# Linear attention and a gated FFN in one Trainium2 kernel: Q's weights loaded as two halves of the rows instead of four quarters, and the first passes of Q0 and Q1 each cut in two

## The chip, the cores and the metric

The kernel runs on one core of a Trainium2 chip. The core has five engines with queues of their own: TensorE (PE in the profile; PEld are its weight loads), VectorE (DVE), ScalarE (ACT), GpSimd (POOL) and SyncE (SP), which here only issues transfers. Each engine works off its own instructions in order; they wait for each other, and for transfers (DMA), by semaphores. The metric is the device time of one execution in microseconds (us), lower is better.

## The reference

One sequence of 2048 tokens with 576 features goes through a layer norm, and the sum of three parts is the output: the input itself, linear attention, and an FFN with a gelu gate. Both inner parts take the same normalised tokens.

```
xn = layernorm(x)                                  # 2048 x 576
q, k, v = split(xn @ wqkv)                         # 32 heads of 18
pq, pk = phi(q), phi(k)                            # phi(t) = t + 1 for t > 0, else exp(t); + 1e-6
num = pq @ (pk^T v);  den = pq . sum(pk) + 1e-6    # per head
out = x + (num / den) @ wo + (gelu(xn @ w_gate) * (xn @ w_up)) @ w_down   # FFN width 4608
```

## The kernel before

The 2048 tokens are 16 tiles of 128. A tile n of x is loaded (`load_x`, L163), its statistics are taken (VectorE's `bn_stats`, L310, and `bn_aggr`, L330; rstd on ScalarE, L334 and L335), it is normalised into `xn` (`ln_norm`, L342 to L351), and brought with features on the partitions into `xnT`, for tiles 0 to 3 by TensorE transposes (L363) and two copies (`tp_copy`, L368: half by ScalarE, half by VectorE), for the others by transposing transfers (`dma_transposes`, L371). Tiles 0 and 1 are transposed first with the mean alone removed, into `xcT`; rstd is multiplied in behind the product (`raw`, L456 and L458). For these two, the normalised tile follows by a transposing transfer as well.

K and Q of a tile (`_Token`, L437) are products of that tile with 576 columns of `wqkv`. The 576 rows of the contraction are four blocks of 128 (index `kt`, 0 to 3) and an end of 64. TensorE runs as two halves of 64 rows, called LO (rows 0 to 63) and HI (64 to 127); each output of 576 columns is two banks of 288 (index `i` below), and each bank gets both halves. `_Unit` (L248) does that in two passes. In the first pass (`rows`, L264) LO works for bank 0 and HI for bank 1, kt 0 to 3: 4 pairs of matmuls. Then the halves swap the banks, which needs a "turn": an empty instruction on GpSimd (`swap`, L270) that waits for the first pass, and for which the second pass (`p2`, L277) waits. The second pass has kt 0 to 3 and the end (kt 4, tile `w_ends`): 5 pairs. All matmuls of these units and of the FFN's units are recorded under L259. The FFN's gate and up products for the first 512 tokens (units g0 to g13, class `_Raw`) are woven into the same stretch, and K4 to K15 follow among them.

Order of the work. The engines' queues are filled by a planner: every piece of work is a `step` (L302) with an engine, an assumed time, a rank, what it comes after, and an earliest time (`ready`); `in_order` (L69) plays them through and emits them in the order in which they begin. TensorE's order is written out by hand in `line` (L493), where `t2` is tile 2's transposes, `K0` and `Q0` are first passes, and a point is the second pass of the oldest unit that has had its first:

```
line = "t0 t1 K0 K1 . . Q0 Q1 . t2 . K2 Q2 . t3 . K3 Q3 .".split()
```

The transfers of SyncE's queue are written out too (the calls at L209 to L223, then `loads`, L597). The planner's assumed landings stand in `X_AT`, `W_AT` and `DMA_FREE` (L373 to L375). `LATER` (L47) is the earliest time at which it plans the exp of the K tiles that were put aside raw (K0, K1, K3), and 16 us after it that of the Q tiles (Q0, Q1, Q3).

Loads at the start. SyncE issues x tile 0, K's weights (`load_w_main(1)`, one load of 128 partitions by 4 blocks by 576 columns), and then Q's weights in four quarters (`load_w_quarter`, L170), each 64 partitions by 4 blocks by 288 columns, x tile 2 between the first and the second. The first two quarters (LO with columns 0 to 287, HI with 288 to 575) are just what a first pass reads, the last two the rest of what a second pass reads. ScalarE issues x tile 1. GpSimd issues the ends of K's weights at once, and the two ends of Q's (`load_w_ends`, L175) as steps behind two small pieces of its own work. x tile 3 follows on SyncE. GpSimd's queue also holds `x_twin` (L354), a copy of a tile's last 64 features that the transposes need, and the two first loads of the FFN's ends (`load_ends`, L191).

After this stretch (to about 57 us) come the Gram product of K (`gram`, L628), the attention matrix, and then four rounds of FFN units, down projection and output.

Of the kernel before, what the change touches and what calls it, by code (L numbers as in the profile page):

```python
# [14 lines left out]
P = 128  # L15
HP = 64
S = 2048
D = 576
# [25 lines left out]
LAG = 0.08  # L44
RAW_T = ("K0", "Q0", "K1", "Q1", "K3", "Q3")
HEAD_T = RAW_T + ("K2", "Q2")
LATER = 40.0  # L47
CENTRED = (0, 1)
LEAD = 5


# [37 lines left out]
def kernel(  # L89
# [73 lines left out]
    def load_x(n0, cnt, on=nc.sync):  # L163
        on.dma_start(x_sb[:, n0:n0 + cnt, 0:D], x_view[:, n0:n0 + cnt, :])  # L164

    def load_w_main(which):
        c = slice(which * D, (which + 1) * D)
        nc.sync.dma_start(wqkv_sb[:, 0:4, c], A_wqkv[0:4 * P, c].rearrange("(kt p) c -> p kt c", p=P))  # L168

    def load_w_quarter(which, rows, half):  # L170
        c = which * D + half * HALF
        view = A_wqkv[0:4 * P, c:c + HALF].rearrange("(kt p) c -> p kt c", p=P)
        nc.sync.dma_start(wqkv_sb[rows, 0:4, c:c + HALF], view[rows])  # L173

    def load_w_ends(which, halves):  # L175
        for i in halves:
            c = which * D + i * HALF
            nc.gpsimd.dma_start(w_ends[(HI, LO)[i], which, :], A_wqkv[512:576, c:c + HALF])

    def load_w_last(which, rows):  # L180
        c = slice(which * D, (which + 1) * D)
# [31 lines left out]
    nc.vector.memset(warm[:], 0.0)  # L213
    nc.vector.memset(x_sb[:, 1, 0:1], 0.0)
    load_x(1, 1, nc.scalar)
    load_w_ends(1, (0, 1))
    load_w_main(1)
    load_w_quarter(0, LO, 0)
    load_x(2, 1)
    load_w_quarter(0, HI, 1)  # L220
    load_w_quarter(0, LO, 1)
    load_w_quarter(0, HI, 0)
    load_x(3, 1)  # L223

    act_acc = const.tile([P, 1], F32, name="act_acc")
# [22 lines left out]
    class _Unit:  # L248
# [12 lines left out]
                start=start, stop=stop, skip_group_check=True,  # L261
            )

        def rows(self):  # L264
            for kt in self.first:
                self.mm(0, LO, kt, kt == self.first[0], False)
                self.last = self.mm(1, HI, kt, kt == self.first[0], False)

# [101 lines left out]
    def dma_transposes(n):  # L370
        nc.sync.dma_start_transpose(xnT[:, :, n * P:(n + 1) * P], xn[:, n, :])  # L371

    X_AT = [3.40, 3.80, 7.30, 9.70]  # L373
    W_AT = {"K": 6.00, "Q": 7.90}
    DMA_FREE = 9.8  # L375

    places = {}

# [4 lines left out]

    for n in range(4, NS, 2):
        load(("x", n), 0.58, 295, 9.0, [], lambda n=n: load_x(n, 2), ready=6.0)
    for half, behind in enumerate((("twin", 1), ("mean", 1))):
        step(("w_ends", half), "POOL", 0.6, -9.0, [behind], lambda half=half: load_w_ends(0, (half,)))
    for part, turn in enumerate(("K1", "Q0")):
        step(("ends", part), "POOL", 0.7, 3.0, [("turn", turn)], lambda part=part: load_ends(0, nc.gpsimd, (part,)))

    for n in range(NS):
        first = 1.5 * n if n < 4 else 9.0 + 3.0 * (n - 4)
        both = n // 2 * 2
        after_x = [("x", both)] if n >= 4 else []
        x_at = X_AT[n] if n < 4 else 12.6 if n < 8 else 2.1 * both + 3.0
        if n < 4:
            step(("twin", n), "POOL", 0.2, first, [], lambda n=n: x_twin(n, 1), ready=10.1 if n == 3 else x_at)
        elif n == both:
            step(("twin", n), "POOL", 0.25, first, after_x, lambda n=n: x_twin(n, 2), ready=max(2.6 * n + 3.0, 14.6))
        twin = ("twin", n if n < 4 else both)  # L400
        if n != 1:
            for h in range(2):
                step(("stats", n, h), "DVE", 0.42, first, after_x + [("xnT", 2, 1)] * (n == 3 and h) + [("phi", "Q2")] * (n in (4, 5)) + [("phi", "K5")] * (n in (12, 13)), lambda n=n, h=h: ln_half(n, h), ready=x_at)
            step(("aggr", n), "DVE", 0.2, first, [("stats", n, 0), ("stats", n, 1)], lambda n=n: ln_aggr(n), tail=0.05)
        if n in CENTRED:
            if n:
                step(("sum", n), "ACT", 0.78, first - 3.0, [], lambda n=n: act_sum(n), ready=x_at)
                step(("mean", n), "POOL", 0.54, first - 3.0, [("sum", n)], lambda n=n: act_mean(n), tail=-0.27)
                step(("aggr", n), "ACT", 0.95, first + 2.0, [("mean", n), ("xnT", 1, 0)], lambda n=n: act_square(n))
            mean = ("mean", n) if n else ("aggr", n)  # L410
            step(("centre", n), "DVE", 0.45, first - 0.5, [mean, twin], lambda n=n: centre(n), tail=0.05)
        if n not in (1, 2) and n < 6:
            step(("rstd", n), "ACT", 0.5, first - 2.0 * (n == 3), [("aggr", n)], lambda n=n: ln_rstd(n, 1))
        elif n == both:
            m = min(n, 1) if n < 6 else n
            step(("rstd", n), "ACT", 0.46, first, [("aggr", m), ("aggr", m + 1)], lambda m=m: ln_rstd(m, 2))
            if n == 2:
                steps[("rstd", 1)] = _Step("none", 0.0, first, [("rstd", 2)], lambda: None, 0.0, 0.0)
        ready = [("rstd", n if n < 6 else both), twin]
        if NORM[n] == "A":  # L420
            step(("bias", n), "POOL", 0.27, first, ready[:1], lambda n=n: ln_bias(n))
            ready.append(("bias", n))
        on, took = ("ACT", 0.92) if NORM[n] == "A" else ("DVE", 0.45)
        if n < HEAD:
            late = n in CENTRED
            step(("norm", n), on, took, 2.5 if late else first, ready + [("tp", n)] * late, lambda n=n: ln_norm(n), tail=0.05)
            step(("tp", n), "PE", 0.2, 0, [("centre" if late else "norm", n)], lambda n=n: transposes(n), tail=0.15)
            for i, copied in enumerate((0.44, 0.30)):
                step(("xnT", n, i), "DVE" if i else "ACT", copied, first - 1.0, [("tp", n)], lambda n=n, i=i: tp_copy(n, i), tail=0.02)
            steps[("xnT", n)] = _Step("none", 0.0, first, [("xnT", n, 0), ("xnT", n, 1)], lambda: None, 0.0, 0.0)  # L430
            if late:
                load(("xnU", n), 1.25, 80, first + 2, [("norm", n)], lambda n=n: dma_transposes(n))
        else:
            step(("norm", n), on, took, first, ready, lambda n=n: ln_norm(n), tail=0.05)
            load(("xnT", n), 1.25, 80, first + 2, [("norm", n)], lambda n=n: dma_transposes(n))
# [54 lines left out]
                out=hT[:, self.f:self.f + NF + 1:NF, :], in_=ps_all[:, self.two[0]:self.two[0] + 2, :],  # L490
            )

    line = "t0 t1 K0 K1 . . Q0 Q1 . t2 . K2 Q2 . t3 . K3 Q3 .".split()  # L493
    follow = [f"g{i}" for i in range(LEAD)]
    for i in range(12):
        follow += [f"K{i + 4}"] + ([f"g{i + LEAD}"] if i + LEAD < RAW else [])
# [27 lines left out]

    def p2_step(u):
        n = int(u.name[1:])
        pe(("p2", u.name), u.t2, [("turn", u.name)], u.unit_p2, ready=9.4 if u.name == "Q0" else 0.0)
        if u.name[0] in "KQ":
            later = u.name in RAW_T
            if later:  # L530
                step(("raw", u.name), *(("DVE", 0.82) if u.name == "Q1" else ("ACT", 0.75 if n < 2 else 0.66)), u.at, [("p2", u.name), ("rstd", n or 2)] + [("norm", 3)] * (u.name == "Q1") + [("xnT", 2, 0)] * (u.name == "Q0"), u.body.raw)
            ready, rank = ((LATER, 60.0) if u.name[0] == "K" else (LATER + 16.0, 70.0)) if later else (0.0, u.at - 3.0 * (u.name == "K4"))
            held = [("xnT", 3, 0)] if u.name == "K2" else []
            step(("exp", u.name), "ACT", 0.70, rank, [("raw" if later else "p2", u.name)] + held, u.body.exp, ready=ready)
            step(("clamp", u.name), "DVE", 0.25, rank + 1, [("exp", u.name)], u.body.clamp)
            step(("phi", u.name), "DVE", 0.76, rank + 1, [("clamp", u.name)], u.body.phi, tail=0.05)
            owner[tuple(u.body.banks)] = [("raw" if later else "phi", u.name)]
        else:
            step(("out", u.name), "ACT", 1.05, u.at, [("p2", u.name)], u.body.out)
            owner[tuple(u.body.two)] = [("out", u.name)]  # L540

    clock = 5.5
    for name in line:
        if name == ".":
            p2_step(pending.pop(0))
            continue
        kind, n = name[0], int(name[1:])
        if kind == "t":
            two = (tp_banks[n], tp_banks[n] + 1)
            steps[("tp", n)].after = steps[("tp", n)].after + owner.get(two, [])  # L550
            pe(("tp", n), 0, [], None)
            owner[two] = [("xnT", n, 0), ("xnT", n, 1)]
            if name == "t0":
                pe("spin", 0.27, [], lambda: row_spin(5))
            continue
        u = _Chain()
        u.name, u.at = name, clock
        if kind in "KQ":
            u.body = _Token(kind, n, head_banks if name in HEAD_T else banks)
            b = u.body.banks  # L560
            after = [("xnT", n)]
            t1, u.t2 = 0.49, 0.615
            u.p1 = u.body.unit.rows
            u.swap = u.body.unit.swap
            u.unit_p2 = u.body.unit.p2
            at = W_AT[kind]
        else:
            u.body = _Raw(n)
            b = u.body.two
# [5 lines left out]
            u.unit_p2 = lambda body=u.body: body.unit.p2()  # L575
            at = 0.0
        after += owner.get(tuple(b), [])
        pe(("p1", name), t1, after, u.p1, ready=at)
        step(("turn", name), "POOL", 0.06, clock, [("p1", name)], u.swap, tail=0.05)
        clock += t1 + u.t2  # L580
        pending.append(u)
    while pending:
        p2_step(pending.pop(0))
# [428 lines left out]
```

## Time and profile before

| | us |
|---|---|
| median of 3 runs (508.46, 509.66, 509.67) | 509.66 |
| the profiled execution, whole | 508.54 |
| its span in the profile | 506.8 |
| TensorE busy in the span | 502.5 |

The profile is one further execution. All times in it count from the start of the span. A row of the timeline gives start and length in us, engine, source line, operation, what it writes from what, shapes and count; in brackets stands how long the engine had been idle before it, and what ended that. "SPq" is the issue of a transfer on SyncE. A row of the windows gives the length of a stretch, each engine's busy time in it, the granted clock of TensorE (1.00 throughout), the share of the transfer engines and GB/s.

### The profile page before, as it was taken

How to read it: one execution, taken by the hardware profiler on the slowest of the kernel's cores; microseconds unless marked ns; L12 is line 12 of the kernel's file. 1: busy time of each engine (PE TensorE's matmuls, PEld its weight loads, DVE VectorE, ACT ScalarE, POOL GpSimd, SP SyncE). 2: the span in 40 equal slices, each digit the busy share in tenths (PEclk: the TensorE clock that was granted, in tenths of full speed). 3: DMA queues.
4: the chain of work that ended last, by engine and by line, in shares of the span. 5: the costliest groups of instructions: out<-in, count | busy, mean ns of one | idle time of the engine just before them, and what ended most of it. 6: DMA issues, size and time to landing. Idle time of an engine off the chain costs nothing.

```text
span 506.8 us, 11207 instructions
## 1 busy us (share of the span) xinstructions
PE 502.5 (99%) x4765; PEld 304.8 (60%) x4765; DVE 230.8 (46%) x481; ACT 150.4 (30%) x263; POOL 11.2 (2%) x36
## 2 busy tenths in 40 slices
PE   9999999999999999999999999999999999999997
PEld 7666784446777444445777444445777444445774
DVE  4779896773002665553002665553102665553100
ACT  5678734325001522332001432333001432232000
POOL 4100100000000000000000000000000000000000
PEclk9999999999999999999999999999999999999999
DMA  9998916993201455653000455653000455640000
GB/s 218 236 240 188 313 51 196 269 258 96 71 13 35 136 152 170 170 153 107 12 13 31 140 151 166 173 155 108 13 12 29 143 149 162 175 107 14 13 12 25
DMA packets 115227, 61.76 MB, mean 122 GB/s; under 512 B 24642, under 2 KB 115082, under 8 KB 115178
## 3 DMA queue, kind: packets, MB, share of 16 engines
q1 hardware_dynamic: 114842, 60.63, 45.6%
q8 instruction: 37, 0.61, 0.5%
q0 software_dynamic: 192, 0.28, 0.2%
q10 hardware_dynamic: 144, 0.15, 0.1%
q14 instruction: 12, 0.10, 0.1%
HBM read 53.60 MB, written 2.36 MB: 110 GB/s over the span
## 4 chain that ended last, share of the span: by engine, by line
PE 97%; DMA 1%; SPq 1%; issue 0%; DVE 0%
PE ps_all L259 62%; PE ps_all L927 28%; PE ps_all L628 3%; PE ps_all L932 3%; DMA wqkv_sb<-in_A_wqkv_dram 1%; PE ps_all L915 0%; PE ps_all L636 0%; SPq L173 0%; PE ps_all L655 0%; SPq L164 0%; PE ps_all L867 0%; SPq L168 0%; PE ps_all L363 0%; DVE res L941 0%; PE ps_all L674 0%
## 5 line engine op out<-in xcount | busy, mean ns | idle before, releaser
L259 PE MATMUL ps_all<-xnT,wg 64*128 64x512 bf16 x1152 | 273.7, 376 | 0.0
L259 PE MATMUL ps_all<-xnT,wu 64*128 64x512 bf16 x1152 | 273.1, 376 | 0.0
L259 PEld LDWEIGHTS <-wg 64*128 64x128 bf16 x1152 | 108.3, 94 | 66.5
L259 PEld LDWEIGHTS <-wu 64*128 64x128 bf16 x1152 | 108.2, 94 | 65.5
L820 DVE TENSOR_TENSOR hT<-ps_all,gl 128x512 bf16<-128x512 f32 x130 | 89.8, 691 | 104.2 <-ACT gl L819 104.1
L927 PEld LDWEIGHTS <-hT 128*128 128x128 bf16 x1152 | 110.8, 98 | 30.9 <-issue 1.3
L819 ACT ACTIVATE gl<-ps_all 128x512 f32<-128x512 f32 x130 | 77.6, 597 | 164.1 <-PE ps_all L259 163.7
L941 DVE TENSOR_TENSOR res<-ps_all,x_sb 128x288 bf16<-128x288 f32 (+2 forms) x32 | 13.8, 455 | 146.3 <-PE ps_all L932 88.1
L927 PE MATMUL ps_all<-wd_a,hT 128*128 128x288 bf16 (+2 forms) x512 | 68.3, 286 | 0.0
L259 PE MATMUL ps_all<-xnT,wr 64*128 64x512 bf16 x288 | 54.9, 376 | 0.0
L927 PE MATMUL ps_all<-hT 128*128 128x288 bf16 (+2 forms) x384 | 52.4, 286 | 0.0
L841 ACT ACTIVATE gl<-ps_all 128x288 f32<-128x288 f32 x24 | 9.2, 410 | 121.4 <-PE ps_all L259 118.9
L927 PE MATMUL ps_all<-wd_m,hT 128*128 128x288 bf16 (+2 forms) x256 | 36.8, 286 | 0.0
L259 PEld LDWEIGHTS <-xnT 64*128 64x128 bf16 x504 | 26.6, 94 | 6.9 <-ACT xnT L368 0.6
L259 PEld LDWEIGHTS <-wr 64*128 64x128 bf16 x288 | 14.2, 94 | 16.3
L932 PE MATMUL ps_all<-m_sb,pqT 128*128 128x288 bf16 (+2 forms) x128 | 20.9, 286 | 0.0
L259 PE MATMUL ps_all<-wqkv_sb,xnT 64*128 64x288 bf16 x256 | 19.7, 283 | 0.1
L628 PE MATMUL ps_all<-hT,xn 128*128 128x288 bf16 x128 | 16.2, 286 | 0.0
L489 ACT CAST hT<-ps_all 128x1024 bf16<-128x1024 f32 x14 | 14.1, 1010 | 4.9 <-PE ps_all L259 4.8
L628 PEld LDWEIGHTS <-xn 128*128 128x128 bf16 x128 | 12.4, 98 | 3.7 <-issue 0.7
L310 DVE BATCH_NORM_STATS2 stats<-x_sb 128x6 f32<-128x288 bf16 x30 | 12.2, 440 | 5.2 <-DMA x_sb<-in_A_x_dram 5.2
L932 PEld LDWEIGHTS <-pqT 128*128 128x128 bf16 x128 | 12.4, 98 | 3.3
(98 smaller groups left out, 246.8 us busy)
## 6 DMA issues: line engine op xcount, KB each, us to landing
wg<-in_B_w_gate_dram SPq DMA_DIRECT2D x72, 256.0 KB, 3.0
wu<-in_B_w_up_dram SPq DMA_DIRECT2D x72, 256.0 KB, 3.6
wd_a<-in_B_w_down_dram SPq DMA_DIRECT2D x4, 576.0 KB, 8.6
wr<-in_B_w_gate_dram SPq DMA_DIRECT2D x35, 64.0 KB, 3.3
wr<-in_B_w_up_dram SPq DMA_DIRECT2D x35, 64.0 KB, 2.9
out_dram<-res SPq DMA_DIRECT2D x15, 144.0 KB, 1.8
x_sb<-in_A_x_dram SPq DMA_DIRECT2D x6, 288.0 KB, 4.9
hT<-in_B_w_down_dram SPq DMA_DIRECT2D x4, 432.0 KB, 5.4
```

Of the source, the lines that this page charges most:

```text
L259: return nc.tensor.matmul(self.outs[i], lhsT=self.lhs(i, rows, kt), rhs=self.rhs(i, rows, kt), start=start, stop=stop, skip_group_check=True,)
L310: nc.vector.bn_stats(out=ln_raw[n][:, h, :], in_=x_sb[:, n, h * HALF:(h + 1) * HALF])
L489: nc.scalar.copy(out=hT[:, self.f:self.f + NF + 1:NF, :], in_=ps_all[:, self.two[0]:self.two[0] + 2, :],)
L628: nc.tensor.matmul(ps_all[:, two[hf], :HALF], lhsT=xn[:, n, kt * P:(kt + 1) * P], rhs=pk[:, n, hf * HALF:(hf + 1) * HALF], start=(n == gra ...
L819: nc.scalar.activation(out=gl[:], in_=ps_all[:, b[0], :], func=ACT.Gelu_apprx_tanh)
L820: nc.vector.tensor_tensor(out=hT[:, GUB * k + i, :], in0=ps_all[:, b[1], :], in1=gl[:], op=ALU.mult)
L841: nc.scalar.activation(out=e[:, :HALF], in_=acc, func=ACT.Exp)
L927: nc.tensor.matmul(self.acc(hf), lhsT=hT[:, f, j * P:(j + 1) * P], rhs=wd(f)[:, self.parts[hf]], start=(f == 0 and not paired), stop=False ...
L932: nc.tensor.matmul(self.acc(hf), lhsT=pqT[:, c, self.ts], rhs=m_sb[:, c, self.parts[hf]], start=False, stop=(paired and c == 3), skip_grou ...
L941: nc.vector.tensor_tensor(out=self.res[:, hs], in0=self.acc(hf), in1=x_sb[:, self.n, hs], op=ALU.add)
```

## The change

Q's weights come as two loads of 128 partitions and 576 columns, kt 0 and 1 in one, kt 2 and 3 in the other. x tile 2 is issued before both, and the two ends of Q's weights after them, on SyncE's queue. As each half holds both banks' columns but only half of the contraction, the first passes of Q0 and Q1 are cut: `Q0a`, `Q1a` take kt 0 and 1, `Q0b`, `Q1b` kt 2 and 3, and tile 2's transposes stand ahead of Q0's second pass instead of behind it. The turns of Q0 and Q1 follow the second halves. GpSimd issues both first loads of the FFN's ends behind K1's turn; the plan's assumed landings and `LATER` have other values, so the planner puts some of VectorE's and ScalarE's work in another order.

```diff
-LATER = 40.0
+LATER = 38.0
+WQ_PARTS = ((0, 1), (2, 3))
...
-    def load_w_main(which):
+    def load_w_main(which, kts=slice(0, 4)):
         c = slice(which * D, (which + 1) * D)
-        nc.sync.dma_start(wqkv_sb[:, 0:4, c], A_wqkv[0:4 * P, c].rearrange("(kt p) c -> p kt c", p=P))
...
+        view = A_wqkv[0:4 * P, c].rearrange("(kt p) c -> p kt c", p=P)
+        nc.sync.dma_start(wqkv_sb[:, kts, c], view[:, kts, :])
+
+    def load_w_ends(which, on):
+        for i, rows in enumerate((HI, LO)):
             c = which * D + i * HALF
-            nc.gpsimd.dma_start(w_ends[(HI, LO)[i], which, :], A_wqkv[512:576, c:c + HALF])
+            on.dma_start(w_ends[rows, which, :], A_wqkv[512:576, c:c + HALF])
...
-    load_w_ends(1, (0, 1))
+    load_w_ends(1, nc.gpsimd)
     load_w_main(1)
-    load_w_quarter(0, LO, 0)
     load_x(2, 1)
-    load_w_quarter(0, HI, 1)
-    load_w_quarter(0, LO, 1)
-    load_w_quarter(0, HI, 0)
+    for kts in WQ_PARTS:
+        load_w_main(0, slice(kts[0], kts[-1] + 1))
+    load_w_ends(0, nc.sync)
     load_x(3, 1)
...
-        def rows(self):
-            for kt in self.first:
+        def rows(self, kts=None):
+            for kt in self.first if kts is None else kts:
...
-    X_AT = [3.40, 3.80, 7.30, 9.70]
-    W_AT = {"K": 6.00, "Q": 7.90}
-    DMA_FREE = 9.8
+    X_AT = [3.40, 3.80, 6.90, 9.60]
+    W_AT = {"K": (6.00,), "Q": (7.90, 8.90)}
+    DMA_FREE = 9.6
...
-    for half, behind in enumerate((("twin", 1), ("mean", 1))):
-        step(("w_ends", half), "POOL", 0.6, -9.0, [behind], lambda half=half: load_w_ends(0, (half,)))
-    for part, turn in enumerate(("K1", "Q0")):
-        step(("ends", part), "POOL", 0.7, 3.0, [("turn", turn)], lambda part=part: load_ends(0, nc.gpsimd, (part,)))
+    for part in range(2):
+        step(("ends", part), "POOL", 0.6, 3.0, [("turn", "K1")], lambda part=part: load_ends(0, nc.gpsimd, (part,)))
...
-    line = "t0 t1 K0 K1 . . Q0 Q1 . t2 . K2 Q2 . t3 . K3 Q3 .".split()
+    line = "t0 t1 K0 K1 . . Q0a Q1a Q0b Q1b t2 . . K2 Q2 . t3 . K3 Q3 .".split()
...
+        if name[-1] == "b":
+            u = pending[-1 if name[:2] == pending[-1].name else -2]
+            pe(("p1", u.name), 0.245, [], lambda u=u: u.p1(WQ_PARTS[1]), ready=W_AT["Q"][1])
+            step(("turn", u.name), "POOL", 0.06, clock, [("p1", u.name)], u.swap, tail=0.05)
+            continue
...
+        if name[-1] == "a":
+            pe(("p1a", u.name), 0.245, after, lambda u=u: u.p1(WQ_PARTS[0]), ready=at)
```

More of the change, by code (lines that the diff above doesn't have):

```diff
@@ L164, in load_x @@
         on.dma_start(x_sb[:, n0:n0 + cnt, 0:D], x_view[:, n0:n0 + cnt, :])
-    def load_w_main(which):
+    def load_w_main(which, kts=slice(0, 4)):
         c = slice(which * D, (which + 1) * D)
-        nc.sync.dma_start(wqkv_sb[:, 0:4, c], A_wqkv[0:4 * P, c].rearrange("(kt p) c -> p kt c", p=P))
[L170 to L176, printed above, removed]
+        view = A_wqkv[0:4 * P, c].rearrange("(kt p) c -> p kt c", p=P)
+        nc.sync.dma_start(wqkv_sb[:, kts, c], view[:, kts, :])
+    def load_w_ends(which, on):
+        for i, rows in enumerate((HI, LO)):
             c = which * D + i * HALF
-            nc.gpsimd.dma_start(w_ends[(HI, LO)[i], which, :], A_wqkv[512:576, c:c + HALF])
+            on.dma_start(w_ends[rows, which, :], A_wqkv[512:576, c:c + HALF])
     def load_w_last(which, rows):
@@ L396 @@
         if n < 4:
-            step(("twin", n), "POOL", 0.2, first, [], lambda n=n: x_twin(n, 1), ready=10.1 if n == 3 else x_at)
+            step(("twin", n), "POOL", 0.2, first, [("turn", "Q1")] * (n == 3), lambda n=n: x_twin(n, 1), ready=10.1 if n == 3 else x_at)
         elif n == both:
@@ L526, in p2_step @@
         n = int(u.name[1:])
-        pe(("p2", u.name), u.t2, [("turn", u.name)], u.unit_p2, ready=9.4 if u.name == "Q0" else 0.0)
+        pe(("p2", u.name), u.t2, [("turn", u.name)], u.unit_p2)
         if u.name[0] in "KQ":
@@ L546 @@
             continue
-        kind, n = name[0], int(name[1:])
+        kind, n = name[0], int(name[1:].rstrip("ab"))
         if kind == "t":
@@ L555 @@
             continue
+        if name[-1] == "b":
[3 more added lines that the diff above has]
+            continue
         u = _Chain()
-        u.name, u.at = name, clock
+        u.name, u.at = name[:2] if name[-1] == "a" else name, clock
         if kind in "KQ":
-            u.body = _Token(kind, n, head_banks if name in HEAD_T else banks)
+            u.body = _Token(kind, n, head_banks if u.name in HEAD_T else banks)
             b = u.body.banks
@@ L565 @@
             u.unit_p2 = u.body.unit.p2
-            at = W_AT[kind]
+            at = W_AT[kind][0]
         else:
@@ L577 @@
         after += owner.get(tuple(b), [])
-        pe(("p1", name), t1, after, u.p1, ready=at)
-        step(("turn", name), "POOL", 0.06, clock, [("p1", name)], u.swap, tail=0.05)
         clock += t1 + u.t2
+        if name[-1] == "a":
+            pe(("p1a", u.name), 0.245, after, lambda u=u: u.p1(WQ_PARTS[0]), ready=at)
+        else:
+            pe(("p1", name), t1, after, u.p1, ready=at)
+            step(("turn", name), "POOL", 0.06, u.at, [("p1", name)], u.swap, tail=0.05)
         pending.append(u)
```

## The prediction

> **What bounds the kernel now.** I read the page's first part, the chain of waits in order of time, the waits of the first 18 us, and the timeline of the first 16 us.
>
> ```profile
> span 506.8 us, 11207 instructions
> PE 502.5 (99%) x4765; PEld 304.8 (60%) x4765; DVE 230.8 (46%) x481; ACT 150.4 (30%) x263; POOL 11.2 (2%) x36
> ```
>
> TensorE (PE) is busy for 99% of the span. The change leaves its instructions in number and shape as they are, so it can only win or lose idle time. The chain (start, length, what) shows where that time is:
>
> ```profile
> 4.46 5.56 DMA wqkv_sb<-in_A_wqkv_dram
> 10.06 0.83 PE ps_all L259 x9
> ...
> 14.30 42.81 PE ps_all L259 x504
> 57.11 3.78 PE ps_all L628 x30
> 60.90 8.25 PE ps_all L628 x66
> ```
>
> Until 10.02 the end hangs on a transfer, the last quarter of Q's weights. From 14.30 PE is one piece but for a hole at 60.7. The weight loads (PEld) say who ended each hole of the head; the columns are total us, times, longest:
>
> ```profile
> PEld L259 <- ACT xnT L368: 0.6, 2, 0.4
> PEld L259 <- issue: 0.6, 2, 0.4
> PEld L259 <- POOLq L270: 0.3, 1, 0.3
> PEld L363 <- DVE xn L348: 0.2, 1, 0.2
> ```
>
> These are weight-load gaps; the matmuls run on through part of each, so they add up to more than PE loses. The pace of undisturbed work comes from the timeline (start, length):
>
> ```profile
> 11.63 1.65 PE L259 MATMUL ps_all<-wqkv_sb,xnT 64*128 64x288 bf16 x24
> ...
> 13.10 0.30 PE L259 MATMUL ps_all<-w_ends,xnT 64*128 64x288 bf16 x2
> ```
>
> Twelve pairs start between 11.63 and 13.10: 0.1225 us a pair. A first pass (4 pairs) is 0.49, a half 0.245, a second pass (5 pairs) 0.61.
>
> **The change, part by part.** *The loads.* Four quarters become two halves; x tile 2 moves ahead of all of them; the ends of Q's weights move from GpSimd to SyncE, behind them.
>
> ```profile
> 1.73 0.74 SPq L173 DMA_DIRECT2D wqkv_sb<-in_A_wqkv_dram  x1
> 2.51 0.59 SPq L164 DMA_DIRECT2D x_sb<-in_A_x_dram  x1
> ...
> 3.15 1.93 SPq L173 DMA_DIRECT2D wqkv_sb<-in_A_wqkv_dram  x3
> ...
> 5.13 0.60 SPq L164 DMA_DIRECT2D x_sb<-in_A_x_dram  x1
> ```
>
> SyncE issues as many as before: four quarters of 0.64 to 0.74 go, two halves and two ends come, near 0.6 each, so x tile 3 still goes out near 5.1. What changes is the rate, in GB/s at the row's end:
>
> ```profile
> 4.00:5.00 1.00, 1.00 (x11) 0.81 (x8) 0.84 (x3) 0.97 (x4) 0.86 (x3) 1.00 1.08 384
> 6.00:9.50 3.50, 3.50 (x62) 2.51 (x58) 1.62 (x5) 1.49 (x4) 0.81 (x3) 1.00 1.16 207
> ```
>
> Between 4 and 5 us K's weights come in, 128 partitions of 1152-byte rows: 384. Between 6 and 9.5 it is the quarters, 64 partitions of 576-byte rows: 207. A half has the shape of K's load. K's issue at 1.27 takes 4.5 us to land:
>
> ```profile
> wqkv_sb<-in_A_wqkv_dram SPq DMA_DIRECT2D x1, 576.0 KB, 4.5
> ```
>
> So K lands at 5.8. Behind it come x2 (147 kB), two halves of 295, the ends (74), x3 (147). At 384 they land at 6.2, 7.0, 7.7, 8.1 (the ends at 207), 8.5; at 207, the other bound, at 6.5, 7.9, 9.4, 9.7, 10.4. A bound below is not reasonable: fewer, longer rows have no row here that runs under 207. I take 384, the row of the same shape.
>
> [...]
>
> *The wait of x2.*
>
> ```profile
> 8.03 0.82 DVE L310 BATCH_NORM_STATS2 stats<-x_sb 128x6 f32<-128x288 bf16 x2 [1.31 <-DMA x_sb<-in_A_x_dram]
> 8.06 0.23 POOL L354 COPY x_sb<-x_sb 128x64 bf16<-128x64 bf16 x1 [2.00 <-PE ps_all L259]
> 8.10 1.58 PEld L259 LDWEIGHTS <-xcT 64*128 64x128 bf16 x28 [0.27 <-POOLq L270]
> ...
> 9.81 0.81 DVE L348 TENSOR_SCALAR xn<-x_sb,mv,rstd 128x640 bf16<-128x640 bf16 x2 [0.72 <-ACT rstd L335]
> ```
>
> VectorE waits for x2 until 8.03. GpSimd's queue has x2's copy in front of K1's turn, so PE waits too: K1's second pass could follow K0's at 7.96 and starts at 8.10. With x2 at 6.2 to 6.5 the statistics start when VectorE is free, at 6.72 (its copy at 6.39 takes 0.32), 1.3 earlier, and norm 2 (the first at 9.81, 0.45 long) ends near 8.95 instead of 10.25.
>
> *PE.* K1's second pass 7.96, Q0a 8.57, Q1a 8.82, Q0b 9.07, Q1b 9.31. The halves are there (7.0 and 7.7; the slow bound, 7.9 and 9.4, is priced below). Tile 2's transposes, 0.15 long, at 9.56 find norm 2 done. Q0's and Q1's second passes take 1.22, to 10.93; the ends, landed at 8.1 to 9.7, are needed at 10.2. K2 and Q2's first passes 0.98, K2's second 0.61, tile 3's transposes 0.15, Q2's second 0.61: K3 at 13.28, against 14.30. That is 4.21 behind the start of Q0b.
>
> *What is late next.* K3 also needs VectorE's copy of tile 3:
>
> ```profile
> 10.54 0.44 DVE L310 BATCH_NORM_STATS2 stats<-x_sb 128x6 f32<-128x288 bf16 x1
> ...
> 11.38 0.75 ACT L456 ACTIVATE pq<-ps_all,rstd 128x576 bf16<-128x576 f32 x1
> ...
> 12.13 0.30 ACT L334 ACTIVATE rstd<-mv,eps_ln 128x1 f32<-128x1 f32 x1
> ...
> 12.75 0.45 DVE L348 TENSOR_SCALAR xn<-x_sb,mv,rstd 128x640 bf16<-128x640 bf16 x1 [0.66 <-ACT rstd L335]
> ...
> 13.11 0.81 DVE L458 TENSOR_SCALAR pq<-ps_all,rstd 128x576 bf16<-128x576 f32 x1
> ...
> 13.84 0.32 DVE L368 COPY xnT<-ps_all 128x320 bf16<-128x320 bf16 x1
> ```
>
> On ScalarE Q0's copy (11.38), then tile 3's rstd, then norm 3, Q1's copy and xnT's on VectorE, then K3: 14.30 − 11.38 = 2.92. The changed order keeps this sequence, and Q0's copy now starts when Q0's second pass has drained, its last pair starts 0.49 behind 9.71 and takes 0.30: 10.5. K3 then starts near 13.45: 0.8 gained, 0.2 of PE's possible 1.0 stays a wait. With the halves at 207 GB/s Q0b waits until 9.44, and K3 is at 9.44 + 4.21 = 13.65: 0.65.
>
> *New waits.* Q0b and Q1b wait for the second half; behind them on PE stands everything. GpSimd issues both first FFN ends between K1's turn (7.56) and Q0's (needed 9.5), two at 0.52 and gaps of 0.3, done by 9.2. K2's turn stands behind x3's copy; x3 has until 11.4. If that cover were gone, each would cost PE one for one.
>
> *LATER 38.* Q0's exp goes ahead of K13's, and its two VectorE steps into a hole:
>
> ```profile
> 56.16 0.62 DVE L468 TENSOR_SCALAR phi_e<-phi_e 128x576 bf16<-128x576 bf16 x1 [1.28 <-ACT phi_e L465]
> ...
> 57.56 0.33 DVE L468 TENSOR_SCALAR phi_e<-phi_e 128x576 bf16<-128x576 bf16 x1
> 57.93 0.76 DVE L474 SCALAR_TENSOR_TENSOR pq<-pq,phi_e 128x576 bf16<-128x576 bf16 x1
> ...
> 60.09 0.76 DVE L474 SCALAR_TENSOR_TENSOR hT<-ps_all,phi_e 128x576 bf16<-128x576 f32 x1
> ```
>
> K15's phi ended at 60.85, and the Gram product waited until 60.90. Its 30 matmuls before that, at 0.1225, could go on at 60.73: 0.17 lost. 0.33 + 0.76 = 1.1 leave the queue ahead of K15's phi, which comes near 59.75, and PE, 0.8 earlier, asks at 59.9. Without this edit the 0.8 would be lost here. I count 0.15 gained; from both sides 0 and 0.17.
>
> **The sum**: 0.8 + 0.15 = 0.95 us. The profiled execution took 508.54 us (span 506.8 and 1.7 around it): 507.6. The executions shown stand in two pairs, 508.46 and 508.54, 509.66 and 509.67; the profiled one is of the lower, the median of the upper, and nothing in this trace shows the 1.15 between. I take the middle of the pairs, 509.1, less 0.95: 508.1.
>
> **Rivals.**
> *The halves land no sooner.* For: the load is shared with whatever else is queued. Against: 384 in the same shape, and fewer bytes ahead. K3 starts 4.21 behind the landing's release; from 10.05 on nothing is left. Before, the last quarter landed at 10.02: gain 0, with the Gram hole 0.15: 509.0.
> *The gain is taken back by weights of the FFN units.* For: PE comes 0.8 sooner to loads at near 290 GB/s:
>
> ```profile
> 10.50:12.50 2.00, 2.00 (x40) 1.55 (x38) 1.38 (x5) 1.89 (x5) 0.23 (x1) 1.00 1.12 290
> ```
>
> Against: these start behind x1's transposing transfer, which waits for norm 1, itself about 1.3 earlier. What is left then is 0 to 0.4: 508.9.
> *Slower: norm 6 behind x8.* In the changed order VectorE's norm 6 stands behind all of x8's first statistics, not behind one half:
>
> ```profile
> 22.76 0.46 DVE L310 BATCH_NORM_STATS2 stats<-x_sb 128x6 f32<-128x288 bf16 x1 [1.45 <-DMA x_sb<-in_A_x_dram]
> 23.14 0.43 DVE L348 TENSOR_SCALAR xn<-x_sb,mv,rstd 128x640 bf16<-128x640 bf16 x1
> ...
> 24.79 2.53 SPq L371 DMA_TRANSPOSE xnT<-xn  x2
> 31.44 0.67 PE L259 MATMUL ps_all<-wqkv_sb,xnT 64*128 64x288 bf16 x8
> ```
>
> Three more steps of 0.45, 0.21 and 0.41 put its end near 24.6 for the same landing, just in time for its transpose at 24.79. It decides from x8 landing about 23: each us beyond holds SyncE's queue, the transposes of 6 and 7 and the weights behind, and K6 at 31.44. Two us cost 509.1 − 0.95 + 2 = 510.2. Against: x8 is issued about a us sooner.
>
> **How the numbers follow.** Forecast 0.71 (own range 507.3 to 509.0: the pair that the median falls in, and 0.65 to 1.0); no sooner 0.10; taken back 0.08; slower 0.11. 0.3% of 509.66 is 1.53, about what a measurement of this kernel can tell from no change: faster means below 508.13. The forecast lies at that edge: a median of the lower pair (507.6) is over it, one of the upper (508.7) is not: 0.36 and 0.35. The two cases of a lost gain are within. Of the slower case 0.03 stays within and 0.08 goes over 511.2, with more than one late landing. Faster 0.36, same 0.56, slower 0.08. The range leaves out the slower case and the ends: 507.3 to 509.7.
>
> **What would show it.** Right: the chain leaves the DMA before 8.6 us; x2's statistics start near 6.7; no wait on GpSimd's turn before K1's second pass; K3 near 13.5, ended by xnT's copy; PE unbroken at the Gram product. Wrong: a matmul of Q0b waiting for a DMA after 9.1 us; PE holes between 15 and 57 us; K3 at 14.3.

## The result and the profile after

The changed kernel takes 507.31 us (median of 10 executions, 507.05 to 507.74), the kernel before, run beside it, 508.44 (10 executions, 507.94 to 509.83). The ratio of the means is 0.9972, 95% interval 0.9962 to 0.9982: a gain of 0.9 to 1.9 us. The executions of before form two groups, seven at 507.94 to 508.88 (median 508.31) and three at 509.66 to 509.83; the changed kernel has one group. So the gain has two parts: 1.0 from the lower group (508.31 to 507.31), and the upper group, which is gone (3 of 10 executions, 1.4 each, 0.4 in the mean).

The page of the changed kernel, first two lines; its profiled execution took 507.23 us.

```profile
span 505.5 us, 11200 instructions
PE 500.9 (99%) x4765; PEld 304.7 (60%) x4765; DVE 230.8 (46%) x481; ACT 150.4 (30%) x263; POOL 10.4 (2%) x34
```

The span is 1.3 shorter. The chain of the changed kernel (start, length, what):

```profile
0.81 2.65 DMA x_sb<-in_A_x_dram
...
5.99 3.45 PE ps_all L255 x52
9.59 2.82 PE ps_all L255 x46
12.55 43.40 PE ps_all L255 x514
55.95 11.87 PE ps_all L630 x96
```

It leaves the DMA with x tile 0, at 3.46, and no longer with Q's weights at 10.02. From 5.99 it stays on TensorE, the Gram product is one piece, and the hole at 60.7 is gone. Who ended TensorE's holes before 18 us in the changed kernel (weight loads; total us, times, longest):

```profile
PEld L359 <- DVE xn L321: 0.6, 1, 0.6
PEld L255 <- ACT xcT L364: 0.2, 1, 0.2
PEld L255 <- ACT xnT L364: 0.2, 1, 0.2
```

No GpSimd turn is left, and no "issue": in the kernel before, those were two waits that ended 0.04 behind the landings of the last quarter (10.02) and of the second end (10.55). The stages of the head, timeline of the changed kernel:

```profile
5.26 0.44 PE L239 MATMUL ps_all<-warm 64*128 64x128 bf16 x10
...
6.35 0.80 DVE L306 BATCH_NORM_STATS2 stats<-x_sb 128x6 f32<-128x288 bf16 x2
6.54 2.59 PEld L255 LDWEIGHTS <-xcT 64*128 64x128 bf16 x44 [0.20 <-ACT xcT L364]
...
7.67 0.67 PE L255 MATMUL ps_all<-wqkv_sb,xcT 64*128 64x288 bf16 x8
...
8.12 0.80 DVE L344 TENSOR_SCALAR xn<-x_sb,mv,rstd 128x640 bf16<-128x640 bf16 x2 [0.72 <-ACT rstd L331]
...
8.28 1.16 PE L255 MATMUL ps_all<-wqkv_sb,xcT 64*128 64x288 bf16 x16
...
10.25 0.74 ACT L450 ACTIVATE pq<-ps_all,rstd 128x576 bf16<-128x576 f32 x1 [0.22 <-PE ps_all L255]
...
13.05 1.49 PEld L255 LDWEIGHTS <-xnT 64*128 64x128 bf16 x26 [0.19 <-ACT xnT L364]
```

These are the ten fillers between the transposes of tiles 0 and 1, x2's statistics, K1's first pass (6.54), K1's second (7.67), norm 1 and 2, the cut first passes of Q0 and Q1 as one run of 16 matmuls from 8.28, Q0's copy, and K3 (13.05). The same three points in the kernel before:

```profile
5.33 0.72 PE L243 MATMUL ps_all<-warm 64*128 64x128 bf16 x10
...
6.83 1.00 PEld L259 LDWEIGHTS <-xcT 64*128 64x128 bf16 x18 [0.26 <-ACT xcT L368]
...
14.27 1.49 PEld L259 LDWEIGHTS <-xnT 64*128 64x128 bf16 x26 [0.39 <-ACT xnT L368]
```

From K1's first pass to K3 it was 7.44 and is 6.51: the head gains 0.93. The other 0.29 of K3's 1.22 was there before any changed transfer mattered: the same ten fillers take 0.72 in one execution and 0.44 in the other (last section).

The rate of the loads in the changed kernel (windows; GB/s at the end):

```profile
4.00:5.00 1.00, 0.63 (x11) 0.46 (x8) 0.85 (x3) 0.97 (x4) 0.39 (x2) 1.00 1.09 389
...
6.00:8.70 2.70, 2.70 (x44) 2.33 (x46) 1.94 (x7) 2.36 (x7) 1.08 (x3) 1.00 1.13 296
```

The halves come at 296, between the quarters' 207 and the 384 of K's load; why not at 384, no run shows.

### The profile page after: what moved, and what is told of

Its sections match the earlier page's. It is cut to its first block, busy times and chain, and to the rows that moved or that the text cites. A ratio compares the mean times of both kernels' runs of the same rounds, so it can differ in the third digit from the quotient of the medians.

```text
span 505.5 us, 11200 instructions
## 1 busy us (share of the span) xinstructions
PE 500.9 (99%) x4765; PEld 304.7 (60%) x4765; DVE 230.8 (46%) x481; ACT 150.4 (30%) x263; POOL 10.4 (2%) x34
## 4 chain that ended last, share of the span: by engine, by line
PE 98%; DMA 1%; DVE 0%; issue 0%; DVEq 0%
PE ps_all L255 62%; PE ps_all L929 28%; PE ps_all L630 3%; PE ps_all L934 3%; DMA x_sb<-in_A_x_dram 1%; PE ps_all L917 0%; PE ps_all L638 0%; PE ps_all L657 0%; PE ps_all L869 0%; PE ps_all L359 0%; DVE stats L306 0%; DVE xn L321 0%; DVE res L943 0%; PE ps_all L239 0%; PE ps_all L676 0%
```

## The experiments

Times are medians of 6 to 12 executions (e6: a single one); ratios are of the means, to the kernel before on the same chip, and so they move with the share of its upper group. The lower group of before has its median at 508.36 beside e1 to e6, e8 and e9, 508.32 beside e10 and e12, 508.41 beside e15, and 508.07 beside e7 and e14.

### One part at a time: LATER, x tile 2, and a first guess at the upper group

**e1**, the kernel before with `LATER`:

```diff
-LATER = 40.0
+LATER = 38.0
```

> The kernel before with LATER at 38 and nothing else. Theory (the prediction's Gram term): the hole at 60.60 to 60.90 closes, worth 0.15 to 0.17; median 508.3 against 508.44, K3 still at 14.30. Rival: K15's clamp is paced by ScalarE and not by the two steps of Q0 in VectorE's queue, so the hole stays, 508.44.

**e2**, the changed kernel with the same line turned back:

```diff
-LATER = 38.0
+LATER = 40.0
```

> The changed kernel with LATER back at 40. Theory A: VectorE's queue moves forward with TensorE, whose banks it waits for (the 1.28 us hole ahead of K13's clamp moves too), so the old hole of 0.17 at the Gram product comes back and no more: 507.5 against 507.31. Theory B, the prediction's sentence that without this edit the head's gain would be lost at the Gram product: VectorE ends K15's phi where it did, and TensorE waits there for all of the 1.2 us that it came sooner: 508.5.

Measured: e1 509.18 (507.88 to 509.75; ratio 0.9997, 0.9986 to 1.0008), six of its 12 at 509.34 and more, which hides a tenth or two. e2 507.59 (507.26 to 508.52; 0.9973, 0.9963 to 0.9983). The chain of e1 has the Gram product whole:

```profile
56.72 11.87 PE ps_all L628 x96
```

The chain of e2 has it in two, with the hole of before:

```profile
55.86 3.78 PE ps_all L630 x30
59.64 0.01 issue
59.65 8.25 PE ps_all L630 x66
```

In the traces `LATER` closes a hole of 0.17 and no more; the times of e1 can't show so little. Theory A of e2 holds, by way of ScalarE: in the kernel before VectorE waits for its exp (1.28 ahead of K13's clamp), and ScalarE, from 50 to 57 us, for TensorE's banks (0.73 and 0.65). So VectorE's queue moved forward with TensorE, and the head's gain isn't lost without the edit. Two executions of e2, at 508.19 and 508.52, lie apart, and no profile shows why.

**e4**, the kernel before with x tile 2 first, and **e8**, with one load of FFN weights sooner:

```diff
+    load_x(2, 1)
     load_w_quarter(0, LO, 0)
-    load_x(2, 1)
```

> The kernel before with x tile 2 issued ahead of all four quarters and nothing else. Theory (the quarters' rate sets the head): the bytes ahead of the last quarter are the same, it lands at 10.0 again, K1's second pass starts at 7.96 instead of 8.10 but Q0's second pass ends at the same time, K3 at 14.2 to 14.3: 508.4, no gain. Rival (the wait for x2 was what mattered, through K1's turn and norm 2): K3 0.3 or more sooner, 508.1 or less.

```diff
-("gu", 2, 0), ("x", 8), ("gu", 2, 1),
+("gu", 2, 0), ("gu", 2, 1), ("x", 8),
```

(e8 also spells out how the planner orders two steps of equal time and rank.)

> The kernel before with the third up load of the FFN's gate and up weights issued ahead of x tiles 8 and 9 (two lines of the transfer list swapped). In the profile of before that load landed at 23.57 and its first matmul started at 23.63, with the load's median engine done at 22.14. Theory S: executions in which one engine's part of this load comes later make the upper group of the times (3 of 10 at 509.66 to 509.83); with the load about 0.9 us sooner the group goes: all executions under 509.2, median 508.3. Rival: the upper group has another cause; about 3 in 10 stay at 509.7, median 508.4.

Measured: e4 508.28 (0.9996, 0.9984 to 1.0007), seven executions at 508.01 to 508.36 and five at 509.46 to 509.60; e8 509.07 (1.0001, 0.9989 to 1.0013), six of 12 at 509.57 to 509.91. Moving x2 alone brings about 0.2 (e4's lower group has its median at 508.12, before's beside it at 508.36), and the FFN load is not what makes the upper group: theory S falls. But e4's profiled execution took 509.60, one of the upper group. Its waits and its chain:

```profile
PEld L259 <- issue: 1.7, 1, 1.7
```

```profile
5.36 6.23 DMA w_ends<-in_A_wqkv_dram
11.59 0.04 issue
11.63 0.30 PE ps_all L259 x2
```

The second end of Q's weights, 36 kB, is issued by GpSimd at 5.36 and lands 6.2 us later. Fifteen of its sixteen parts, one for each transfer engine, are there by 10.0; the last comes at 11.59. The transfer queues of that execution between 9.7 and 10.8 (packets, MB, share of 16 engines):

```profile
q8 instruction: 1, 0.02, 6.0%
```

One packet of the instruction queue, and 6.0% of 16 engines' 1.1 us is 1.06 us: it is on one engine for that time, from 9.72 to 10.77. That the end's last part waits behind it is inferred from these times; the part lands 0.8 after the packet's end, and what holds it so long stays open. No execution of the kernel before itself was profiled in the upper group. The page of before counts these packets too:

```profile
q8 instruction: 37, 0.61, 0.5%
```

To each of the 37 packets there come 16 kB of these 0.61 MB, and 258 of TensorE's 2 x 4765 instructions (matmuls and weight loads). That the packets bring TensorE's instructions, about 64 bytes each, is my estimate from these three numbers; a count further down bears on it.

### The ends of Q's weights

**e9**, the kernel before with the ends on SyncE, behind the quarters:

```diff
     load_w_quarter(0, HI, 0)
+    load_w_ends(0, nc.sync)
     load_x(3, 1)
...
-    for half, behind in enumerate((("twin", 1), ("mean", 1))):
-        step(("w_ends", half), "POOL", 0.6, -9.0, [behind], lambda half=half: load_w_ends(0, (half,)))
```

> The kernel before with the two ends of Q's weights issued by SyncE between the last quarter and x tile 3, and nothing else. In an execution of the kernel with x tile 2 first that took 509.6, TensorE waited for the second end until 11.59: the last of its engines came 1.7 us behind the median one (9.90), after a 16 kB packet of the instruction queue that began at 9.72, when x tile 3 had landed, and took 1.05 us. Theory I: that packet, queued behind x tile 3 and ahead of an end issued at 5.4, makes the upper group of the times; with the ends ahead of x tile 3 the upper group goes, all executions under 509.2, median 508.3, the lower group where it was. Rival: the packet strikes x tile 3 or a quarter instead, an upper group stays, median 508.4 to 508.8.

Measured: 509.13, all 12 at 508.72 to 509.40 (0.9998, 0.9986 to 1.001). Theory I as I had put it, the packet queued behind x tile 3, is wrong, and so is the rival. SyncE issues the second end at 5.88 here, later than GpSimd did, and now every execution is struck, by its time. The chain of e9:

```profile
5.88 5.23 DMA w_ends<-in_A_wqkv_dram
11.11 0.04 issue
```

From e4 and e9 (second ends issued at 5.36 and 5.88, landed at 11.59 and 11.11) I took it that the packet has its place in time, near 5.4 to 5.9, and that a transfer issued behind that waits on one engine. The next runs put this to the test.

**e10**, the kernel before without the ten fillers (20 instructions of TensorE), and **e15**, the same cut in e9:

```diff
-                pe("spin", 0.27, [], lambda: row_spin(5))
+                pe("spin", 0.27, [], lambda: row_spin(0))
```

> The kernel before without the ten filler matmuls that TensorE runs between the transposes of tiles 0 and 1 (they feed nothing), so that its stream has 20 instructions fewer (weight loads among them); transfers and all else as before. The 16 kB packets of the instruction queue are 37 in 508 us, 0.61 MB, as many bytes as TensorE's 9530 instructions at 64 bytes each. Theory T: the first of them is asked for when TensorE reaches a certain place in its stream, near 5.4 us, beside the issue of the second end at 5.46; with 20 instructions fewer TensorE reaches the place half a us later, while t1 or K0 runs, the end is ahead of the packet in every execution, and the upper group goes: all under 509.2, median 508.3. Rival: another engine's stream or a fixed time sets the packet, 4 in 10 stay near 509.7.

> The kernel before with the ends of Q's weights on SyncE between the last quarter and x tile 3 (which put every execution at 508.72 to 509.40, the instruction packet in front of the second end) and without the ten filler matmuls between the transposes of tiles 0 and 1. Theory T (TensorE asks for the packet at a certain place of its stream): the request comes half a us or more later, behind the second end's issue at 5.88, the end lands near 9.8 in all executions and TensorE's wait of 1.4 us for it goes: all under 508.7, median 508.2, unless the packet strikes x tile 3, issued at 6.4, which would show as a late landing of that tile and not of the end. Rival (a fixed time or another engine sets the packet): 508.7 to 509.4 again, the second end landing at 11.1.

Measured: e10 508.40 (0.9992, 0.998 to 1.0004), one of 12 in the upper group, where the kernel before had 5 of 23 beside it: too few to tell. e15 508.58 (0.999, 0.9974 to 1.0006), in two groups of six, 507.96 to 508.28 and 508.88 to 509.47. Its profiled execution (509.47) has another transfer struck, as theory T allowed. The chain of e15:

```profile
6.35 0.49 SPq L178
6.84 0.04 issue
6.88 4.92 DMA x_sb<-in_A_x_dram
```

The end issued at 6.35 isn't waited for, and x tile 3, issued at 6.88, lands at 11.81. Nothing but TensorE's stream was shortened, and the packet began at 9.54 instead of 8.46 in e9, and struck what was issued behind the end. (K's weights landed 0.5 later in this execution and held up SyncE's issues by as much; the packet moved by 1.1.)

One begin alone doesn't tell when a packet was asked for: in e10, which also has 20 instructions fewer, it begins at 10.20, in before at 10.35. A count over all 37 packets does. When packet k (from 0) begins, TensorE has begun 256 k instructions and some more. The smallest such surplus is 147 or 148, and the median one 160 to 168, in every one of the fifteen profiles, e10 and e15 among them. If the time or another engine set the packets, these two would show some 20 less. So it is TensorE's place in its stream that asks for them.

**e12**, the changed kernel with the ends back on GpSimd in their old places (no `load_w_ends(0, nc.sync)`, the two steps of e9's diff back in), and **e7**, with them on GpSimd at once:

```diff
-    load_w_ends(0, nc.sync)
+    load_w_ends(0, nc.gpsimd)
```

> The changed kernel with the ends of Q's weights back on GpSimd, behind x1's copy and behind x1's mean as before, so that the second is issued near 5.4 again. Theory I (the instruction packet, asked for near 5.4, holds one engine for 1.6 us): the ends land near 8.9 in one group of executions and near 10.5 in another, of 4 in 10 or so; TensorE asks for them at 9.90, so the upper group is 0.6 above the lower one: 507.3 and 507.9, median 507.4 to 507.7. Rival: the move of the ends did nothing for the time, one group at 507.3.

> The changed kernel with the ends of Q's weights issued by GpSimd right behind the ends of K's, near 2.6 and 3.1 us, and not by SyncE. With the ends on GpSimd in their old places the time was 506.86, 0.45 under the changed kernel, though TensorE's last product starts only 0.04 sooner: SyncE has two transfers fewer, and at the end of the program it waits for eight transfer semaphores in a fixed order, 0.062 apart, which its transfers use in turn; the last output uses the second of them in the kernel before and in the changed one, and the eighth with two transfers fewer, so that six waits stand ahead of that landing instead of behind it. Theory: 506.85 again, and, since both ends are far ahead of the instruction packet of 5.4 us, no group above it (all under 507.3 but for odd ones). Rival for the 0.45 (the ends were late or disturbed x tile 3 on SyncE's queue): 507.3.

Measured: e12 506.86 (0.9969, 0.9958 to 0.998), eight executions at 506.78 to 506.92 and four at 507.08 to 507.60: two groups, as theory I said, but both some 0.4 lower; e7 506.99 (0.996, 0.9946 to 0.9975), all at 506.70 to 507.11 (in its profile the ends share the halves' time, and TensorE waits for the second half until 8.88). The upper group by the time at which the second end is issued (an execution counts as struck by its time; profiles of struck ones are those of e4, e9 and e15):

| kernel | second end issued, us | executions struck |
|---|---|---|
| e7 | 3.04 | 0 of 8 |
| changed | 3.87 | 0 of 10 |
| e1, e4, e8 | 5.36 to 5.45 | 17 of 36 |
| before, e12 | 5.43 to 5.46 | 3 of 10 (47 of 125 over all runs of before, four of them at 511.26 to 511.75, apart from the group), 4 of 12 |
| e9 | 5.88 | 12 of 12 |

In the changed kernel, then, the group is gone because the second end goes out well ahead of the packet. Of e2, e3 and e14, which issue it by 4.0, three executions of 28 lie apart, without a profile.

### The last half microsecond

e12 and e7 are faster than the changed kernel, which was not foreseen for e12. The end of the program shows why, for most of it. SyncE's wait for the last output: changed kernel, e12, and e14 (below).

```profile
SPq L1009 <- DMA out_dram<-res: 1.1, 1, 1.1
```

```profile
SPq L1010 <- DMA out_dram<-res: 0.6, 1, 0.6
```

```profile
SPq L1011 <- DMA out_dram<-res: 0.7, 1, 0.7
```

SyncE's transfers use eight semaphores in turn, and at the end it waits for all eight in a fixed order, 0.062 apart. In the kernel before and the changed one the last output has the second of them: one wait, the landing, then six waits more. In e12 and e7, with two transfers fewer on SyncE, it has the eighth, and the others are done while the output travels. **e14** tests that the other way round, with six transfers more:

```diff
-        nc.sync.dma_start(wo2[:CR, 0:4, :], A_wo[0:4 * CR, :].rearrange("(c p) j -> p c j", p=CR))
-        nc.sync.dma_start(wo2[:D - 4 * CR, 4, :], A_wo[4 * CR:D, :])
+        for c in range(4):
+            nc.sync.dma_start(wo2[:CR, c, :], A_wo[c * CR:(c + 1) * CR, :])
+        for c in range(0, D, 144):
+            nc.sync.dma_start(wo2[:D - 4 * CR, 4, c:c + 144], A_wo[4 * CR:D, c:c + 144])
```

> The changed kernel with six transfers more on SyncE: the two loads of the output weights, near 100 us, are cut into four each (the same bytes). Theory (the order of the waits at the end): the last output uses the eighth semaphore, six waits of 0.062 go from behind its landing to ahead of it, and the kernel is 0.37 faster with six transfers more: 506.9. Rival (fewer transfers on SyncE, or the place of the ends, made the 0.45): 507.3 or a little more.

Measured: 506.73 (506.65 to 506.95; 0.9958, 0.9942 to 0.9974), 0.58 under the changed kernel, and the lowest median of all. The last VectorE step and the span, changed kernel and e14:

```profile
span 505.5 us, 11200 instructions
...
502.46 0.29 DVE L943 TENSOR_TENSOR res<-ps_all,x_sb 128x128 bf16<-128x128 f32 x1 [1.61 <-PE ps_all L934]
```

```profile
span 505.2 us, 11208 instructions
...
502.52 0.29 DVE L945 TENSOR_TENSOR res<-ps_all,x_sb 128x128 bf16<-128x128 f32 x1 [1.61 <-PE ps_all L936]
```

From the end of the last step to the end of the span: 2.75 in the changed kernel, 2.4 in e14. The last output is the same; 0.37 is six waits. The other 0.2 goes with the chip, as far as its few executions of before tell: their lower group is 0.24 lower beside e14 than beside the changed kernel. Against the lower group beside it, the changed kernel gains 1.0, e14 1.3, e12 1.5 and e7 1.1. e7 has the same six waits saved, of which its wait for the second half takes back 0.1; the rest of its shortfall is open.

### The halves and the cut

**e3**, the changed kernel with whole first passes:

```diff
-    line = "t0 t1 K0 K1 . . Q0a Q1a Q0b Q1b t2 . . K2 Q2 . t3 . K3 Q3 .".split()
+    line = "t0 t1 K0 K1 . . Q0 Q1 t2 . . K2 Q2 . t3 . K3 Q3 .".split()
```

> The changed kernel with the first passes of Q0 and Q1 whole again (Q0 Q1 t2 in TensorE's order; loads, ends and LATER as changed). In the changed kernel the second half landed at 8.24 and TensorE came to Q0's first pass at 8.28, so both halves are there before the first of them is asked for. Theory: the cut does nothing, 507.3 (within 0.15), no hole at 8.3 or only 0.1. Rival: in other executions the second half lands later than in the profiled one, and the cut covers that: 507.6 or more, and a wider spread.

**e5** and **e6**, the halves by partitions and by columns (`load_w_main` gives way to these):

```diff
+    for rows in (LO, HI):
+        nc.sync.dma_start(wqkv_sb[rows, 0:4, 0:D], wq_view[rows])
```

```diff
+    for c in (0, HALF):
+        nc.sync.dma_start(wqkv_sb[:, 0:4, c:c + HALF], wq_view[:, :, c:c + HALF])
```

> The changed kernel with the two halves cut by partitions: partitions 0 to 63 in one load, 64 to 127 in the other, each with rows of 1152 bytes; all else as changed. Theory P (the number of partitions sets the rate, 207 GB/s for 64 of them in the profile of before): the halves land near 7.6 and 9.0 instead of 7.2 and 8.2, the first pass of Q0 waits 0.7, K3 near 13.8, 508.0. Theory R (the length of the rows sets it, 576 bytes in the quarters and 1152 here): they land as in the changed kernel, K3 at 13.1, 507.3.

> The changed kernel with the two halves cut by columns: 128 partitions each, rows of 576 bytes; all else as changed. Theory P (partitions): they land near 7.2 and 8.2 as in the changed kernel, K3 at 13.1. Theory R (row length): near 7.6 and 9.0, K3 near 13.8.

Measured: e3 507.28 (0.9969, 0.9956 to 0.9982; 11 of 12 at 507.11 to 507.80, one at 508.98), the same as with the cut, so the cut does nothing that these times show. e5 508.42 (0.9985, 0.9972 to 0.9997), e6 507.40 in a single execution. The windows of e5 and of e6:

```profile
6.00:8.70 2.70, 2.58 (x37) 2.02 (x37) 1.41 (x5) 1.62 (x6) 1.13 (x3) 1.00 1.10 202
```

```profile
6.00:8.70 2.70, 2.70 (x41) 2.09 (x42) 1.89 (x7) 2.25 (x7) 1.13 (x3) 1.00 1.21 290
```

With 64 partitions and rows of 1152 bytes 202 GB/s, as the quarters had; with 128 partitions and rows of 576 bytes 290, near the changed kernel's 296. Here the partitions set the rate and the length of the rows next to nothing: theory P holds, R falls; but P's sizes were too small, 9.0 for the landing of e5's second load and 508.0 for its time. In e5 TensorE waits for the second load until 9.85, and K3 is 1.5 later: with all else changed, the slower loads put the time back to that of before's lower group (508.36 beside it).

## Why the prediction was wrong, point by point

**The step that failed is the base.** The prediction said that the executions stand in two pairs, that nothing in the trace shows the 1.15 between, and took "the middle of the pairs, 509.1, less 0.95": it treated the upper pair as a shift that the changed kernel would have as well, and so gave "within 0.3%" the larger chance. The runs showed (the profile of e4, and what e9, e7 and e12 did to the groups) that the upper pair is a wait of TensorE in the head, for the second end behind an instruction packet, and that the change takes it away. Without the middle the forecast would have been 507.6, by its own sum, for 507.31 measured. The same step set the bar: 0.3% of the upper pair's 509.66 was called about what a measurement can tell from no change, but ten executions of each kernel told 0.28% from none, with an interval of 0.1% to either side. That 507.31 still lies in the range, at its very lower end, comes from laying the range over both pairs.

**The move of the ends was costed at nothing.** The prediction asked when they land behind the change (8.1 to 9.7, needed at 10.2), and not when they land before. There the second lands at 10.55 even in the profiled execution, of the lower pair, and of the two "issue" waits in the prediction's list one is TensorE's wait for it:

```profile
10.59 0.09 PEld L259 LDWEIGHTS <-xcT 64*128 64x128 bf16 x1 [0.17 <-issue]
```

In e4's struck execution it landed at 11.59. A struck execution of before is 1.4 longer, 0.4 in the mean of all. The move doesn't bring all of that: with the halves in and the ends in their old places (e12) the struck ones are 0.3 to 0.8 above the others, and with the ends on SyncE the changed kernel lacks the 0.37 that e12 saves at its end.

**The sum for the lower group was nearly right.** 0.95 was said; 508.31 to 507.31 is 1.0. In the traces: head 0.93 for 0.8, Gram 0.17 for 0.15, less 0.06 between K3 and the Gram product. K3 was put at 13.45 and came at 13.08, of which 0.29 is the earlier start of K1's first pass.

**Loads.** x2 lets VectorE begin at 6.35, put at 6.72; the turn of K1 waits no more. The halves' rate was put at 384 with 207 as the other bound, and is 296. It cost nothing: they are there when TensorE asks at 8.28, cut or whole (e3). At the 64-partition rate it would have: e5.

**What is late next.** As said, Q0's copy and then xnT's: K3's weights still wait for the copy, 0.19 by the row above.

**LATER.** The 0.15 is right (0.17 in e1 and e2). "Without this edit the 0.8 would be lost here" is wrong: e2 loses 0.28 in the median, 0.17 of it in the hole.

**Rivals.** The halves land sooner; one TensorE piece from 12.55 to 55.95 shows no wait for FFN weights and none behind norm 6. None of the three came.

What stays open: between which two instructions TensorE asks for the packet, and what holds the struck part on its engine beyond the packet's end.

## What to carry to other kernels

When a few executions differ by a fixed amount, treat that as a wait with a place, and ask what each edit does to it, before taking a middle. A transfer that TensorE needs soon should be issued ahead of the place where its stream asks for the next 16 kB of instructions, since the last part of a transfer behind that came 1.6 us late here. Load with all 128 partitions where you can (290 to 296 GB/s here, against 202 to 207 with 64), and look at which of the eight semaphores the last output has before chasing the last tenths.

## What the runs showed of the hardware that was not expected

- One instruction packet of 16 kB took 1.06 us of one of the 16 transfer engines (e4), and the last part of a 36 kB transfer came 1.6 us behind the other fifteen. The packets keep step with TensorE's stream, one for each 256 of its instructions (37 packets to 9530 instructions; packet k begins when 256 k and, in the kernel before, 148 to 252 more have begun).
- The order of eight waits at the end of the program was worth 0.37 us; six transfers more made the kernel faster.
- TensorE's first matmuls ran at half pace for a time that differed from execution to execution. In the changed kernel's trace the 36 warm-up matmuls, from 1.06 on, start 0.107 apart until 4.0 and 0.056 apart from there; in before's all 36 are 0.107 apart, and the ten fillers took 0.72 against 0.44 (0.72 in e4 as well, 0.44 in e12 and 0.45 in e9), with a granted clock of 1.00 shown for both. It moves K1's first pass by 0.29. The half pace ends 3.0 us behind the first matmul in the one and 4.7 or more in the other; what ends it, no run shows.
